# Token softmax on loaded phi, loads in another order, one more chunk by seven products, and weight sums without a wait

## The chip, the cores and the metric

The kernel runs on one NeuronCore of a Trainium2 chip. The time is that of the device for one execution, in microseconds; the median of three runs is given with the lowest and the highest. TensorE (PE) multiplies, ScalarE (ACT), VectorE (DVE) and GpSimd (POOL) do the rest, SyncE (SP) and ScalarE issue the transfers. Each of these queues is worked through in order.

## The reference

Memory attention of 4 batches, 8 heads, 576 tokens and 64 dims with 32 memory slots, then two feed-forward layers over 2304 tokens:

```python
a = exp(phi - max(phi, axis=2)); a = a / (sum(a, axis=2) + 1e-9)      # softmax over the 576 tokens
k_m, v_m = a^T k, a^T v                                               # 32 x 64 a head
attn = softmax(q k_m^T / 8) v_m                                       # softmax over the 32 slots
x = attn with its heads side by side                                  # 2304 x 512
x = ((x w_a) * (x w_b)) w_out                                         # d_ff 1536
h = x w_in; out = (h * sigmoid(1.702 h)) w_out2                       # d_ff 2048
```

All inputs are float32. The kernel gets its precision from pairs: each operand is split into a rounded part and the rest, and a product is three matmuls (`PASSES`).

## The kernel before, in words

An order planner (`Order`, lines 101 to 192) writes the program. Each piece of work is a generator that asks for an engine, with the time at which its inputs are there and an estimated length, or for a buffer slot, or waits for a mark. The planner takes the request that can start first and, among equal ones, the lowest priority number, and so fixes the order of every engine's queue and of the transfers. Estimated lengths are in `Lengths`, `dve`, `act`, `pool`; the estimated landing of a load is in `load` with `RATE0` (bytes per ns, and a delay) and a start value. What the chip then waits for are semaphores between real accesses.

**Units.** There are eight units of attention (batch and half of the heads, four heads each). `memory(n)` (from line 525) takes phi as loaded, tokens on partitions, five columns of tokens (the fifth half full). It brings phi to the layout with (head, slot) on partitions: for units 0 and 1 by 20 small products with the identity (line 552), for the others by a copy into `et` (lines 540, 542) and five transposes (line 549). There it takes the maximum (lines 556 to 560), the exponential with its sum (lines 562 and 566), transposes back (lines 570, 574), copies into `phi`, and multiplies with k and v (line 590). The sum's reciprocal scales the result (lines 597 to 606), line 612 transposes it, and line 629 makes the scores, whose softmax over slots is `softmax`. `queries` (line 509) transposes q.

**First layer.** `fold` (line 792) multiplies the value memories into groups of w_a and w_b, `gated` (line 844) applies that to the attention weights. A fold needs both units of its batch and four weight pieces. The pieces come as `raw` transfers in the order `FIRST`, into six buffers, and are decoded by ScalarE (lines 438, 442) and VectorE (line 444), which frees the buffer. `warm_up` (line 1582) fills TensorE with products of the identity until the first weight group is there. Line 1006 is the product with w_out by Strassen-like sums (seven products instead of eight), line 1281 that with w_in in the same way.

**Last stage.** The 2304 tokens go in nine chunks of 256. Chunks 0 to 3 are plain (`proj2`, line 1482): 2 tiles x 16 weight chunks x 3 passes, 512 columns each. Chunks 4 to 8 go by seven products (`proj2_seven`, line 1513): 7 x 8 x 3 matmuls of 256 columns, in the order P4, P1, P2, P5, P7, P6, P3. For these, `sums_gated` adds blocks of the gated tokens before splitting them, and `load_pair` (line 1445) loads the decoded w_out2 again, makes four differences T1 to T4 for each of eight pairs and splits them. `load_pair` waits for the mark `decoded`, set when all sixteen weight chunks are ready. P4, P5, P7 and P6 use the T blocks, the other products the chunks themselves. The gated tokens of a plain chunk come in quarters (`f_s`), those of a chunk by seven in halves (`fw_s`); the splits go through a ring of six buffers (`sb_s`). Lines 339 and 345 are helpers that record a difference (VectorE or GpSimd) and a rounding copy (ScalarE) for all of these.

## Time and profile before

| | us |
|---|---|
| median of three runs (lowest to highest) | 745.47 (744.72 to 747.44) |
| the profiled execution | 744.51 |
| its span, first to last instruction | 742.7 |
| TensorE busy | 732.1 |
| VectorE, ScalarE, GpSimd busy | 533.2, 430.8, 386.1 |
| granted TensorE clock, mean share of full | 0.999 |

The span is what the trace shows; the execution's time has some 1.8 us around it. Busy TensorE includes the filler products of the first 29 us. The stages end by their lines as follows: folds and gated products at 242 us, line 1006 at 376 us, line 1281 at 551 us, plain chunks at 638 us, chunks by seven at 739 us.

### The profile page before, as it was taken

What the parts mean: (1) busy time and instruction counts of PE and PEld (TensorE: products, weight loads), DVE (VectorE), ACT (ScalarE), POOL (GpSimd) and SP (SyncE); (2) the same over time, 40 slices, a digit from 0 to 9 for tenths busy, and PEclk for the clock granted to TensorE, in tenths of its full rate; (3) what the DMA queues carried; (4) which work ended last, traced back from release to release, by engine and by line L of the source; (5) the groups of instructions that cost most, each with busy time, mean ns of one, the idle gap of its engine ahead of it and who ended that gap; (6) DMA issues with size and microseconds to landing.
All of it is one profiled execution on the core that took longest, in us unless ns stands there. A gap on an engine that the chain in (4) does not pass through costs nothing.

```text
span 742.7 us, 14507 instructions
## 1 busy us (share of the span) xinstructions
PE 732.1 (99%) x5344; PEld 682.7 (92%) x5344; DVE 533.2 (72%) x799; ACT 430.8 (58%) x842; POOL 386.1 (52%) x347
## 2 busy tenths in 40 slices
PE   9899999999999999999999999999999999999997
PEld 8787888888889999999999999999998888999997
DVE  2987777568983447945898666666665697898884
ACT  3678664667863456546866655565656654544441
POOL 0324366447996616914998621333240296776660
PEclk9999999999999999999999999999999999999999
DMA  8998954786778966676525575544699954544411
GB/s 276 343 327 254 322 190 160 224 280 231 256 237 264 313 195 170 171 211 191 186 100 163 180 227 162 163 136 150 210 377 301 328 157 138 189 143 143 143 26 33
DMA packets 110359, 153.53 MB, mean 207 GB/s; under 512 B 8400, under 2 KB 89040, under 8 KB 110288
## 3 DMA queue, kind: packets, MB, share of 16 engines
q1 hardware_dynamic: 104928, 143.13, 60.3%
q10 hardware_dynamic: 5360, 9.47, 3.9%
q8 instruction: 42, 0.69, 0.4%
q14 instruction: 29, 0.24, 0.1%
HBM read 100.01 MB, written 52.56 MB: 205 GB/s over the span
## 4 chain that ended last, share of the span: by engine, by line
PE 92%; DMA 3%; POOL 2%; DVE 2%; SPq 1%; issue 0%; ACT 0%; DVEq 0%; POOLq 0%
PE bank L1281 24%; PE bank L844 21%; PE bank L1006 16%; PE bank L1513 14%; PE bank L1482 12%; PE bank L792 3%; DMA q<-in_q_dram 1%; PE bank L590 1%; DMA raw_p<-in_moe_w_b_dram 1%; DMA kv<-in_k_dram 1%; PE bank L509 1%; POOL w L339 1%; SPq L372 1%; POOL attn L339 1%; DVE attn L339 0%
## 5 line engine op out<-in xcount | busy, mean ns | idle before, releaser
L844 PEld LDWEIGHTS bank<-attn,eff 128*128 128x128 f32 x1152 | 154.3, 188 | 16.2 <-issue 6.1
L844 PE MATMUL bank<-attn,eff 128*128 128x288 f32 x1152 | 163.1, 298 | 0.5 <-DVE eff L812 0.5
L339 POOL TENSOR_TENSOR acc<-acc 128x512 f32<-128x512 f32 (+2 forms) x65 | 95.0, 1481 | 68.2 <-DVE w L339 27.9
L1323 DVE TENSOR_TENSOR acc<-bank,acc 128x384 f32<-128x384 f32 x168 | 89.8, 553 | 46.3 <-PE bank L1281 40.8
L339 DVE TENSOR_TENSOR w<-acc,w 128x512 fp32r<-128x512 f32 (+2 forms) x100 | 105.0, 1076 | 20.5 <-ACT w L345 20.4
L345 ACT ACTIVATE w<-acc 128x512 fp32r<-128x512 f32 (+2 forms) x129 | 74.9, 590 | 65.7 <-PE bank L1513 38.9
L345 ACT ACTIVATE attn<-acc 128x768 fp32r<-128x768 f32 (+2 forms) x80 | 61.0, 769 | 54.5 <-PE bank L1006 38.7
L1006 PE MATMUL bank<-attn,w 128*128 128x384 f32 x504 | 91.8, 335 | 0.8 <-DVE attn L339 0.7
L1006 PEld LDWEIGHTS bank<-attn,w 128*128 128x128 f32 x504 | 87.5, 188 | 2.0 <-DVE attn L339 1.4
L339 DVE TENSOR_TENSOR attn<-acc,attn 128x768 fp32r<-128x768 f32 (+2 forms) x54 | 65.6, 1225 | 31.9 <-ACT attn L345 30.8
L1333 ACT ACTIVATE acc<-acc 128x384 f32<-128x384 f32 x96 | 49.3, 524 | 44.0 <-DVE acc L1323 43.0
L339 POOL TENSOR_TENSOR attn<-acc,attn 128x768 fp32r<-128x768 f32 (+2 forms) x26 | 41.9, 1623 | 35.8 <-ACT attn L345 35.8
L1281 PE MATMUL bank<-attn,w 128*128 128x384 f32 x288 | 55.1, 334 | 0.0
L339 POOL TENSOR_TENSOR w<-dm,w 128x256 fp32r<-128x256 f32 x27 | 24.5, 908 | 57.9 <-ACT w L345 57.9
L888 POOL TENSOR_TENSOR gr<-gr 128x288 f32<-128x288 f32 x48 | 44.6, 931 | 17.0 <-issue 7.0
L339 POOL TENSOR_TENSOR w<-acc,w 128x256 fp32r<-128x256 f32 (+2 forms) x27 | 30.0, 1119 | 44.4 <-ACT w L345 44.3
L1281 PEld LDWEIGHTS bank<-attn,w 128*128 128x128 f32 x288 | 50.4, 188 | 0.0
L1006 PE MATMUL bank<-attn,w1b 128*128 128x384 f32 x252 | 47.6, 336 | 0.2 <-DVE attn L339 0.2
L339 POOL TENSOR_TENSOR sT<-sT,sm 128x576 f32<-128x576 f32 (+1 forms) x12 | 13.5, 1126 | 64.0 <-DVE sm L654 31.7
L1281 PE MATMUL bank<-w1b,w 128*128 128x384 f32 x224 | 46.2, 334 | 0.0
L1006 PEld LDWEIGHTS bank<-attn,w1b 128*128 128x128 f32 x252 | 43.8, 188 | 0.9 <-DVE attn L339 0.5
L1281 PE MATMUL bank<-w 128*128 128x384 f32 x224 | 43.8, 334 | 0.0
(185 smaller groups left out, 1448.9 us busy)
## 6 DMA issues: line engine op xcount, KB each, us to landing
acc<-g1d SPq DMA_DIRECT2D x63, 384.0 KB, 3.8
g2d<-acc SPq DMA_DIRECT2D x96, 192.0 KB, 2.0
raw<-in_moe_w_out_dram SPq DMA_DIRECT2D x24, 512.0 KB, 4.9
acc<-g2d SPq DMA_DIRECT2D x10, 1024.0 KB, 7.6
raw<-in_moe_w_in_dram SPq DMA_DIRECT2D x16, 512.0 KB, 4.3
acc<-g2d SPq DMA_DIRECT2D x16, 512.0 KB, 5.5
g1d<-gr SPq DMA_DIRECT2D x12, 576.0 KB, 4.9
g1d<-acc SPq DMA_DIRECT2D x8, 576.0 KB, 4.8
```

Source lines behind the costliest of these rows:

```text
L339: (nc.gpsimd if e == POOL else nc.vector).tensor_tensor(out=dst, in0=in0, in1=in1, op=op)
L345: nc.scalar.activation(out=hi, in_=src, func=AF.Copy)
L372: nc.sync.dma_start(out=dst.rearrange("p (n f) w -> p n (f w)", n=runs), in_=src)
L792: nc.tensor.matmul(ps[c][0][row(h), :], bdv[b][half, h, :], wt["wab", g, h][0][half, :], start=True, stop=True)
L844: nc.tensor.matmul(dst[:, :U], e[:, c, sw, i * CW + j * P:i * CW + (j + 1) * P], attn(b, mv, c, u * U, U), start=(n == 0), stop=(n == 3 * ...
L888: nc.gpsimd.tensor_tensor(out=dst, in0=in0, in1=in1, op=ALU.subtract)
L1006: nc.tensor.matmul(ps[0][:, :N2], w1_of(a, g, sw)[:, r * P:(r + 1) * P], b[0][:, mv, i], start=(first and q == n == 0), stop=(q == NG1 // ...
L1281: nc.tensor.matmul(ps[0][:, :N2], w[:, sw, r, :], y[mv][r], start=(n == 0), stop=(n == 5))
L1323: nc.vector.tensor_tensor(out=s[0], in0=ps[0][:, :N2], in1=x[0], op=ALU.add)
L1333: nc.scalar.activation(out=c[0], in_=c[0], func=AF.Gelu_apprx_sigmoid)
L1482: nc.tensor.matmul(ps[i, s][0], b[0][:, sw, c - o, :], wo2[c][:, mv], start=(c == n == 0), stop=(c == 4 * K4 - 1 and n == 2),)
L1513: nc.tensor.matmul(ps[name][0][:, :NB], x[0][:, sw, c, :], moving(b, h // 2 + c, mv), start=(h == c == n == 0), stop=(h > 0 and c == K4 - ...
```

## The change

The softmax over tokens stays in the loaded layout: VectorE takes the maximum over the five columns (`mc`, 128 x 128), TensorE transposes it, VectorE reduces it over tokens, makes a diagonal of its negative, and TensorE multiplies a matrix of ones with that diagonal, so that every partition holds the negative maxima. VectorE adds them to phi into `et`, ScalarE takes the exponential in place, VectorE or GpSimd sums over the columns, and TensorE sums over partitions with a product of one column. k and v are multiplied with `et`. The unused half column of `phi` is filled with -3e38 once. `FIRST` and the planner's landing estimate change; chunk 3 goes by seven products; the pairs' sums no longer wait for `decoded`, at a lower priority.

```diff
--- before.py
+++ after.py
@@ -23,7 +23,7 @@
 W1 = 0.0
 HOLD = {}
 PR = 30
-PT = 28
+PT = 31
 MBN = 8
 PA = 10
 HOLDD = {4: ("attn", 1, 0)}
@@ -35,7 +35,7 @@
 PS1 = 14.8
 PT1 = 15
 FRONT = 1.0, 1.0, 1.0
-RATE0 = 300.0, 2500.0
+RATE0 = 335.0, 1700.0
 RATE = 330.0, 3000.0
 PB1 = 4
 PI = 9
@@ -44,11 +44,12 @@
 PW = 5.5
 PY = 5
 RX = 12
+LEAST = -3.0e38
 
 FIRST = (
     ("phi", 0), ("phi", 1), ("kv", 0), ("q", 0), ("kv", 1), ("q", 1), ("raw", 0), ("raw", 1), ("raw", 2), ("raw", 3),
-    ("raw", 4), ("raw", 5), ("phi", 2), ("kv", 2), ("q", 2), ("raw", 6), ("raw", 7), ("phi", 3), ("kv", 3), ("q", 3),
-    ("raw", 8), ("raw", 9), ("raw", 10), ("raw", 11), ("phi", 4), ("kv", 4), ("q", 4), ("phi", 5), ("kv", 5), ("q", 5),
+    ("raw", 4), ("raw", 5), ("phi", 2), ("raw", 6), ("raw", 7), ("kv", 2), ("q", 2), ("raw", 8), ("raw", 9), ("raw", 10),
+    ("raw", 11), ("phi", 3), ("kv", 3), ("q", 3), ("phi", 4), ("kv", 4), ("q", 4), ("phi", 5), ("kv", 5), ("q", 5),
 )
 
 
@@ -114,7 +115,7 @@
 
     def __init__(self):
         self.clock = {PE: 0.0, ACT: 0.0, DVE: 0.0, POOL: 0.0}
-        self.dma, self.marks, self.streams, self.count = 2000.0, {}, [], 0
+        self.dma, self.marks, self.streams, self.count = 2800.0, {}, [], 0
 
         self.handicap = {DVE: W0}
         self.rate, self.land = RATE0
@@ -306,10 +307,12 @@
     zero = pa.tile([P, 1], F32, name="zero")
     bdk = [pa.tile([P, HG * M], F32, name=f"bdk{i}") for i in range(2)]
     phi_s = slots(pa, 2, [P, HG, C0, M], "phi")
-    et_s = slots(pa, 2, [P, C0, SP, 2], "et")
+    et_s = slots(pa, 2, [P, HG, C0, M], "et")
+    mc_s = slots(pa, 2, [P, HG * M], "mc")
+    ones = pa.tile([P, P], F32, name="ones")
     kv_s = slots(pa, 2, [P, 2, HG, C0, D], "kv")
     q_s = slots(pa, 2, [P, QC, D], "q")
-    mx_s = slots(pa, 3, [P, 6], "mx")
+    mx_s = slots(pa, 3, [P, 2], "mx")
     kvn_s = slots(pa, 2, [P, 2, 2, D], "kvn")
     qT_s = slots(pa, 2, [P, HG, U], "qT")
     sT_s = slots(pa, 2, [P, S], "sT")
@@ -528,82 +531,62 @@
         if n in HOLD:
             yield ("mark", *HOLD[n])
         ph = loaded.pop(("phi", n))
...
+        mc = yield "slot", mc_s
+        t, mx = yield DVE, max(t, mc[1]), dve(HG * C0 * M), mx_s
+        m = [mx[0][:, i:i + 1] for i in range(2)]
+        top = mc[0].rearrange("p (h m) -> p h m", h=HG)
+        nc.vector.reduce_max(out=top, in_=ph[0].rearrange("p h c m -> p h m c"), axis=AX.X)
+        t, bb = yield PE, t, 110, bank_a
+        tp, low, kvp, total = (bb[0][:, i * P:(i + 1) * P] for i in range(4))
+        nc.tensor.transpose(tp, mc[0], ident)
+        t, _ = yield DVE, t, dve(P)
+        nc.vector.reduce_max(out=m[0], in_=tp, axis=AX.X)
+        t, _ = yield DVE, t, dve(P)
+        nc.vector.tensor_scalar(out=mc[0], in0=ident, scalar1=m[0], scalar2=-1.0, op0=ALU.mult, op1=ALU.mult)
+        t, _ = yield PE, t, 220
+        nc.tensor.matmul(low, ones, mc[0], start=True, stop=True)
         et = yield "slot", et_s
...
+        t, _ = yield DVE, max(t, et[1]), dve(HG * C0 * M)
+        nc.vector.tensor_tensor(
+            out=et[0], in0=ph[0],
+            in1=low.rearrange("p (h u m) -> p h u m", h=HG, u=1).to_broadcast([P, HG, C0, M]), op=ALU.add,
         )
...
+        phi_s.release(ph, t)
+        t, _ = yield ACT, t, act(HG * C0 * M)
+        nc.scalar.activation(out=et[0], in_=et[0], func=AF.Exp)
+        t2, e = yield {DVE: dve(HG * C0 * M), POOL: pool(4 * P)}, t
+        if e == DVE:
+            nc.vector.reduce_sum(out=top, in_=et[0].rearrange("p h c m -> p h m c"), axis=AX.X)
+        else:
+            for c in range(1, C0):
+                nc.gpsimd.tensor_tensor(
+                    out=top, in0=et[0][:, :, c], in1=et[0][:, :, 0] if c == 1 else top, op=ALU.add
+                )
+        t = max(t, (yield "mark", "kv", n))
         kvs = loaded.pop(("kv", n))
...
         for c in range(C0):
             t, _ = yield PE, t if c == 0 else 0.0, 240
             for h in range(HG):
                 nc.tensor.matmul(
...
+                    kvp[h * M:(h + 1) * M, :], et[0][:, h, c, :], kvs[0][:, :, h, c, :],
                     start=(c == 0), stop=(c == C0 - 1),
                 )
...
+        et_s.release(et, max(t, t2))
         kv_s.release(kvs, t)
+        t2, _ = yield PE, t2, 110
+        nc.tensor.matmul(total[:, :1], mc[0], ones[:, :1], start=True, stop=True)
+        mc_s.release(mc, t2)
         t2, _ = yield DVE, t2, 70
...
+        nc.vector.tensor_scalar_add(m[1], total[:, :1], 1e-9)
         t2, _ = yield DVE, t2, 75
...
+        nc.vector.reciprocal(out=m[1], in_=m[1])
         kvn = yield "slot", kvn_s
         t, e = yield {ACT: act(256, True), DVE: dve(320)}, max(t, t2, kvn[1])
         kv2 = kvp.rearrange("p (i u d) -> p i u d", i=2, u=1).to_broadcast([P, 2, 2, D])
         if e == ACT:
...
+            nc.scalar.activation(out=kvn[0], in_=kv2, func=AF.Copy, scale=m[1])
         else:
...
+            nc.vector.tensor_scalar(out=kvn[0], in0=kv2, scalar1=m[1], scalar2=None, op0=ALU.mult)
         bank_a.release(bb, t)
         mx_s.release(mx, t)
         t, ps = yield PE, t, 220, bank_a
@@ -1194,7 +1177,7 @@
         yield "mark", "front"
         wide = views(acc, 2 * FN, 3, n)
         give(fw_s, wide[:2])
-        yield "mark", "sw", NQ, 0, A22
+        yield "mark", "sw", NF, 0, A22
         give(fw_s, wide[2:])
         for p in range(F2 // P // 2):
             yield "mark", "wt", p
@@ -1338,7 +1321,7 @@
 
 
 
-    NF, NQ, NS, NW = 3, 4, 4, NT // NB
+    NF, NW = 3, NT // NB
 
     def gated_part(s, i, o, e):
         t = 0.0
@@ -1354,13 +1337,12 @@
         loaded["f", i, o] = s, f
 
     QUARTERS = [(i, o) for o in range(0, 4 * K4, K4) for i in range(NF)]
-    QUARTERS += [(i, o) for i in range(NF, NQ) for o in range(0, 4 * K4, K4)]
 
     def load_gated():
         for i, o in QUARTERS:
             s = yield "slot", f_s
             yield from gated_part(s, i, o, o + K4)
-        for i in range(NQ, NW):
+        for i in range(NF, NW):
             for o in (0, 2 * K4):
                 s = yield "slot", fw_s
                 yield from gated_part(s, i, o, o + 2 * K4)
@@ -1384,20 +1366,8 @@
                 t = max(t, (yield "mark", "sb", i, o, s))
             f_s.release(slot, t)
         od.mark(t, "front")
-        for i in range(NQ, NW):
-            yield from (split_whole(i) if i < NS else sums_gated(i))
-
...
     A21 = 7
     MERGE = {
@@ -1447,7 +1417,7 @@
             in_=w2d[2 * p * P:(2 * p + 2) * P, :].rearrange("(k p) f -> p k f", p=P),
         )
         od.load(max(t, m[1]), 2 * P * DM * 4, "pair", p)
-        t = max((yield "mark", "pair", p), (yield "mark", "decoded"))
+        t = yield "mark", "pair", p
         b11, b12, b21, b22 = (x[:, k, j] for k in range(2) for j in range(2))
         n = DM // 2
         for i, (dst, in0, in1) in enumerate(
@@ -1495,7 +1465,7 @@
 
     def proj2_seven(i):
 
-        if i == NS:
+        if i == NF:
             for p in range(2 * K4):
                 yield "mark", "wt", p
         ps, ts = {}, {}
@@ -1606,7 +1576,7 @@
         od.spawn(9, room_last())
         yield from proj2([(i, s) for i in range(NF) for s in range(2)])
         for i in range(NF, NW):
-            yield from (proj2([(i, 0), (i, 1)]) if i < NS else proj2_seven(i))
+            yield from proj2_seven(i)
 
     def quad(g, p):
         for name in ("P1", "P6", "P7", "P5", "P3", "P4", "P2"):
@@ -1615,9 +1585,10 @@
     with tc.manual_schedule():
 
         last = C0 - 1
-        unused = [s[0][:, :, last, :] for s in phi_s.free] + [s[0][:, last] for s in et_s.free]
-        unused += [s[0][:, i, :, last, :] for s in kv_s.free for i in range(2)]
-        for t in [zero, *unused]:
+        for s in phi_s.free:
+            nc.vector.memset(s[0][:, :, last, :], LEAST)
+        nc.vector.memset(ones, 1.0)
+        for t in [zero] + [s[0][:, i, :, last, :] for s in kv_s.free for i in range(2)]:
             nc.vector.memset(t, 0.0)
         make_identity(nc, ident)
         n0 = 2 * NHG
```

## Rows read from the trace of the kernel before

**Rows 1.** The page, part 1: busy us, share of the span, instructions of each engine.
```profile
...
PE 732.1 (99%) x5344; PEld 682.7 (92%) x5344; DVE 533.2 (72%) x799; ACT 430.8 (58%) x842; POOL 386.1 (52%) x347
...
```

**Rows 2.** The page, part 4: the chain that ended last, share by line.
```profile
...
PE bank L1281 24%; PE bank L844 21%; PE bank L1006 16%; PE bank L1513 14%; PE bank L1482 12%; PE bank L792 3%; DMA q<-in_q_dram 1%; PE bank L590 1%; DMA raw_p<-in_moe_w_b_dram 1%; DMA kv<-in_k_dram 1%; PE bank L509 1%; POOL w L339 1%; SPq L372 1%; POOL attn L339 1%; DVE attn L339 0%
...
```

**Rows 3.** TensorE's waits: line, released by which: us in total, times, longest.
```profile
...
PE bank L549 <- POOL et L540: 1.7, 1, 1.7
...
PE bank L509 <- ACT qT L330: 1.2, 1, 1.2
PE bank L1006 <- DVE attn L339: 0.9, 3, 0.5
PE bank L844 <- DVE eff L812: 0.5, 1, 0.5
...
```

**Rows 4.** The chain in order of time: start us, us, what.
```profile
...
64.95 0.55 PE bank L549 x5
65.50 0.44 PE bank L570 x4
...
66.72 0.11 PE bank L574
...
550.67 87.08 PE bank L1482 x384
637.75 100.80 PE bank L1513 x840
...
```

**Rows 5.** TensorE's instructions in order of time: start us, us, instruction, count.
```profile
...
24.55 4.06 PE L1582 MATMUL bank<-ident 128*128 128x128 f32 x34
...
33.33 3.40 PE L844 MATMUL bank<-attn,eff 128*128 128x288 f32 x24
...
39.83 1.30 PE L590 MATMUL bank<-kv,phi 128*32 128x128 f32 x40
...
```

**Rows 6.** Windows: busy us (instructions) of each engine, clock, DMA share, GB/s.
```profile
...
0.00:29.00 29.00, 27.64 (x361) 25.01 (x364) 14.05 (x43) 14.04 (x33) 2.42 (x8) 1.00 0.91 303
29.00:62.00 33.00, 29.11 (x327) 22.38 (x321) 29.77 (x69) 25.21 (x57) 10.90 (x13) 1.00 0.96 316
551.00:573.00 22.00, 22.00 (x99) 18.19 (x98) 10.22 (x16) 10.90 (x20) 0.90 (x1) 1.00 0.97 316
573.00:594.00 21.00, 21.00 (x94) 17.41 (x93) 13.38 (x21) 13.78 (x28) 4.67 (x6) 1.00 0.97 332
594.00:616.00 22.00, 22.00 (x99) 18.22 (x98) 20.83 (x25) 13.02 (x33) 20.90 (x24) 1.00 0.52 149
...
658.00:678.00 20.00, 20.00 (x169) 20.00 (x168) 17.22 (x21) 8.96 (x16) 13.40 (x9) 1.00 0.47 143
...
```

**Rows 7.** VectorE's groups by shape: busy us, mean ns of one, idle before.
```profile
...
L659 DVE TENSOR_REDUCE sm<-sT 128x18 f32<-128x576 f32 x6 | 4.5, 750 | 1.3 <-ACT sT L657 1.1
...
L558 DVE TENSOR_REDUCE mx<-bank 128x1 f32<-128x64 f32 x8 | 1.6, 204 | 0.0
...
```

**Rows 8.** SP's queue in order of time, as in rows 5.
```profile
...
23.00 0.61 SPq L354 DMA_DIRECT2D kv<-in_k_dram  x1
...
```

**Rows 9.** VectorE in order of time, as in rows 5.
```profile
...
24.46 0.69 DVE L444 SCALAR_TENSOR_TENSOR acc<-acc,raw 128x512 uint32<-128x512 uint32 x1
...
38.42 0.69 DVE L444 SCALAR_TENSOR_TENSOR acc<-acc,raw_p 128x512 uint32<-128x512 uint32 x1 [0.40 <-ACT raw_p L442]
...
```

**Rows 10.** GpSimd in order of time, as in rows 5; idle time before it in brackets.
```profile
...
588.12 1.44 POOL L339 TENSOR_TENSOR acc<-acc 128x256 f32<-128x256 f32 x2 [24.91 <-DVE acc L339]
...
620.66 3.82 POOL L339 TENSOR_TENSOR w<-raw,w 128x256 fp32r<-128x256 f32 x4
...
```

**Rows 11.** Line 1445: ns min/median/max, first and last start.
```profile
...
L1445 ACTq EVENT_SEMAPHORE  x9: 17/38/3898, 552.4 to 606.6; - x9
...
```

**Rows 12.** Groups of lines between 573 and 594 us, columns as in rows 7.
```profile
...
L339 DVE TENSOR_TENSOR w<-acc,w 128x512 fp32r<-128x512 f32 x6 | 4.1, 686 | 1.4 <-ACT w L345 1.4
...
```

**Rows 13.** Groups of lines between 594 and 616 us, columns as in rows 7.
```profile
...
L339 DVE TENSOR_TENSOR w<-acc,w 128x512 fp32r<-128x512 f32 x8 | 9.2, 1146 | 1.2 <-ACT w L345 1.2
...
```

More of the change, by code (lines that the diff above doesn't have):

```diff
@@ L543, in memory @@
-        part = 240 if n < NHG else 70
-        t, ba = yield PE, t, part * last, bank_a
-        t1, bb = yield PE, t, part, bank_a
-        for c in range(C0):
-            dst = (ba if c < last else bb)[0][:, c % last * P:(c % last + 1) * P]
-            if n >= NHG:
-                nc.tensor.transpose(dst, et[0][:, c].rearrange("p s x -> p (s x)"), ident)
-                continue
-            for h in range(HG):
-                nc.tensor.matmul(dst[h * M:(h + 1) * M, :], ph[0][:, h, c, :], ident, start=True, stop=True)
@@ L553, in memory @@
-        even = bb[0][:, :P].rearrange("p (s x) -> p s x", x=2)[:, :, 0]
-        t, mx = yield DVE, t, dve(512), mx_s
-        m = [mx[0][:, i:i + 1] for i in range(6)]
-        nc.vector.reduce_max(out=m[0], in_=ba[0], axis=AX.X)
-        t, _ = yield DVE, max(t, t1), dve(64)
-        nc.vector.reduce_max(out=m[1], in_=even, axis=AX.X)
-        t, _ = yield DVE, t, 70
-        nc.vector.tensor_scalar(out=m[2], in0=m[0], scalar1=m[1], scalar2=-1.0, op0=ALU.max, op1=ALU.mult)
-        t, _ = yield ACT, max(t, et[1]), act(512, True) + 190
@@ L562, in memory @@
-        nc.scalar.activation(
-            out=et[0][:, :last].rearrange("p c s x -> p (c s x)"), in_=ba[0], func=AF.Exp, bias=m[2], accum_out=m[3]
-        )
-        t2, _ = yield ACT, t, act(64, True) + 190
-        nc.scalar.activation(out=et[0][:, last, :, 0], in_=even, func=AF.Exp, bias=m[2], accum_out=m[4])
-        t, _ = yield PE, t, 70 * last
-        for c in range(last):
-            nc.tensor.transpose(
-                ba[0][:, c * P:(c + 1) * P], et[0][:, c].rearrange("p s x -> p (s x)"), ident
-            )
@@ L585, in memory @@
+        t = max(t, (yield "mark", "kv", n))
         kvs = loaded.pop(("kv", n))
-        kvp = bb[0][:, 2 * P:3 * P]
         for c in range(C0):
@@ L603, in memory @@
         if e == ACT:
-            nc.scalar.activation(out=kvn[0], in_=kv2, func=AF.Copy, scale=m[5])
+            nc.scalar.activation(out=kvn[0], in_=kv2, func=AF.Copy, scale=m[1])
         else:
-            nc.vector.tensor_scalar(out=kvn[0], in0=kv2, scalar1=m[5], scalar2=None, op0=ALU.mult)
+            nc.vector.tensor_scalar(out=kvn[0], in0=kv2, scalar1=m[1], scalar2=None, op0=ALU.mult)
         bank_a.release(bb, t)
@@ L1386, in split_gated @@
         od.mark(t, "front")
[L1387 to L1400 removed]
+        for i in range(NF, NW):
+            yield from sums_gated(i)
     A21 = 7
```

36 lines of the change are left out of this document (removed).

## The prediction

> **What bounds the kernel now.** I read the page's busy times first, then the chain that ended last, then who waited, and only then the stretches that the change touches. TensorE is busy for 732.1 of 742.7 us [rows 1], and the chain runs over its lines almost alone [rows 2], so what counts is TensorE work taken out and TensorE waits put in. Those waits are small [rows 3]: 1.7 us just before the first gated product at 33.33 us, 1.2 and 0.5 at lines 509 and 844 in the stretch 29 to 62, 0.9 at line 1006 in the middle. The chain in order of time [rows 4] gives the two pieces of the last stage whole: 87.08 us for 384 matmuls of four plain chunks, 100.80 us for 840 of five chunks by seven products, both without a gap. Ahead of 33.33 us TensorE mostly fills time: the 34 rows of line 1582 are products of the identity that nothing reads [rows 5]. That front ends with vector work. Two stretches are crowded beside TensorE [rows 6]: from 29 to 62 us VectorE is busy 29.77 of 33 us with the DMA engines at 0.96, and from 594 to 616 us VectorE 20.83 and GpSimd 20.90 of 22 us. Between 551 and 594 us it is the other way: GpSimd does 5.6 us in 43, VectorE 23.6, and the DMA engines are at 0.97.
>
> **The change, part by part.** The base is the profiled execution's own 744.51 us (span 742.7 and 1.8 around it), 0.96 under the median of 745.47.
>
> *Chunk 3 by seven products.* A plain chunk is 87.08 / 384 = 226.8 ns a matmul, times 96 = 21.77 us. A chunk by seven is 100.80 / 840 = 120.0 ns, times 168 = 20.16 us [rows 4]. Gain 1.61 us, all on the path as long as the chunk's operands are there. The Trainium skill, "TensorE: Matmul & The Clock Gate", section "Back-to-back issue gap", gives an isolated matmul its columns over 2.4 GHz and 2.5 ns. By that the chunk would gain 96 x 215.8 - 168 x 109.2 = 2.4 us; the rows have about 13 ns over the columns in both forms, and decide.
>
> *The token softmax without transposes.* For units 2 to 7 ten transposes each go: 0.55 us at line 549, 0.44 and 0.11 at lines 570 and 574 [rows 4], 6 x 1.10 = 6.60 us. The first five of unit 2 stand in the front's wait and give nothing, which leaves 6.05. Added for each unit: one transpose, 0.11; one full-precision product with the diagonal, two rows of the kind of line 1582 at 4.06 / 34 = 0.119 [rows 5], 0.24; one product of a single column with the same 128 x 128 weights. No row shows that one: between nothing and the 0.24 of the full product; I take 0.20, near the upper end, since the weights are the same size. Sum 0.55 x 6 = 3.3 us. Net gain 6.05 - 3.3 = 2.75 us (2.5 to 3.9). It counts where TensorE has no gaps, from 33 us on. Units 0 and 1 lose 40 matmuls and ten transposes in the front, where fillers take their place: nothing.
>
> *The vector work that comes for it.* A unit now costs VectorE a maximum over 640 values, one over 128, a scalar operation of 128 columns, an addition of 640 and a sum of 640 (or four additions on GpSimd). The nearest rows are 0.75 us for a reduction of 576 and 0.20 for one of 64 [rows 7]. So 0.82, 0.27, 0.25, 0.82, 0.82 = 3.0 us, and if reading every fifth value of a strided line costs twice as much 4.6; at the low end a sum on GpSimd leaves 2.2. What goes is a reduction of 512 and one of 64, a scalar operation and some of the copies, about 1.4. So VectorE gains 0.8 to 3.2 us a unit, while ScalarE loses two accumulator reads, one exponential and copies, about 1 us. The cover is ScalarE, which can take over copies, and GpSimd, busy 10.90 of 33 us [rows 6]. Without it, two units at 1.6 us in a stretch with 3.2 us of free VectorE put some 3 us on TensorE. I take 0, as the row of GpSimd is the larger room.
>
> *The front.* The chain of units 0 and 1 no longer goes through 20 small products, a read of PSUM by ScalarE and two copies back, and VectorE is busy only 14.05 of the first 29 us [rows 6]; the scores of these two units, and with them the softmax that keeps VectorE full up to the first gated product, can come earlier. The reciprocal now stands behind the products with k and v and one more product, some 0.4 us in the chain. The limit is weight piece 3, whose decode decides the first fold. The gated start at 33.33 can move by 3 us at the most (the wait of 1.7 and about as much of filler) and back by 2 (three or four of the new VectorE operations in front of the fold's). I take 1 us earlier.
>
> *The order of loads.* Weight pieces 6 and 7 now stand on SP's queue ahead of unit 2's k, v and q. Piece 6 reuses the buffer of piece 0, whose last read is VectorE at 24.46 to 25.15; the queue issued unit 2's k at 23.00 [rows 8, 9]. So SP waits up to some 2 us with k, v and q of unit 2 queued behind it; TensorE read them at 39.83 [rows 5]. Pieces 10 and 11 need the buffers of pieces 4 and 5, the latter read at 38.42 to 39.11 [rows 9], and hold back phi, k, v and q of unit 3. Against that, the third group of weights arrives sooner, and TensorE has a third block with the tokens at hand. Between a gain of 1.7 us (the waits of lines 509 and 844 gone) and a loss of as much I take 0. No engine but SP is held.
>
> *Sums of the second output weights early.* The eight pairs cost 32 subtractions and 32 splits. Their last lower part ends at 620.66 + 3.82 = 624.5 [rows 10], 13.3 us before TensorE reaches the first chunk by seven at 637.75. Now TensorE gets there after 288 plain matmuls, at 550.67 + 65.3 = 616.0, less the 3.75 us gained ahead: 612.2. So the sums must move by some 12 us relative to the work around them. Room: GpSimd's idle 37 us and VectorE's 19 between 551 and 594 [rows 6] for 64 operations of 0.7 to 1.2 us, some 60; half of them done there bring the end to about 606. The f loads for chunk 3 come when the ring of six split buffers lets the last plain quarter go, as far ahead of use as before. Each pair's load is issued from ScalarE's queue and waits there for its buffer, up to 3.9 us [rows 11]; splits of f and decodes stand behind it. The ring of six splits holds 6 x 12 x 0.227 = 16 us of TensorE work, which covers one such hold-up. Once chunks by seven run, each keeps VectorE 17.22 and GpSimd 13.40 of 20 us [rows 6], so a sixth one holds its pace. I take 0, with a loss of up to 10 us at the other end.
>
> Sum: 1.61 + 2.75 + 1.0 = 5.4 us. 744.5 - 5.4 = **739.1 us**.
>
> **The rivals.** *The sums come too late.* Place: the start of chunk 3 at 612 us. For: before, GpSimd stood idle for 25 us up to 588 with pairs loaded, since its next sum waited for one on VectorE [rows 10]; both engines were full until the end; and the subtractions of the splits took 686 ns beside an idle GpSimd, 1146 ns beside a busy one [rows 12, 13]. Waking GpSimd up early would stretch the 37 VectorE operations between 551 and 594 us [rows 6] by about 0.46 each, 17 us, and leave VectorE no room: all 64 then take GpSimd's time, about 1 us each from 562, to 626 us, less 3.75 gained ahead: 622. TensorE would stand 10 us and more: 739.1 + 10 to 12 = 749 to 751. The Trainium skill states the mechanism in "SBUF — State Buffer", section "Who interferes with whom": a VectorE instruction with two inputs in SBUF and a GpSimd instruction that reads SBUF exclude each other. By that rule this rival is the likelier; the trace agrees on the stretching, but GpSimd's and VectorE's work did overlap in time at the longer durations. Against: only products P4, P5, P7, P6 need these sums, and P1 and P2, which don't, stand between. It decides from a stall of 5.4 us, an end at about 618.
>
> *VectorE becomes the bound in the front.* For: 29.77 of 33 us busy. The added work costs 3 us between 29 and 62, or the order of loads costs 2, and the front gains nothing: 744.5 - 4.4 + 3 = 743 us. Within 0.5%.
>
> *The front gives all it has.* First gated product at 30.3, waits of 1.7 us gone: 744.5 - 4.4 - 3 - 1.7 = 735 us.
>
> *The change does not reach the path.* The queues' order is written anew from changed costs, and other waits of the middle (0.9 us before line 1006) grow by the 4.4 us that the parts bring: 744.5, within 0.5%.
>
> **How the numbers follow.** Forecast 0.51 (range of its own 736.5 to 742.5), VectorE in the front 0.16, gains lost in the middle 0.10, sums late 0.12, the front gives all 0.11. A run of this kernel can tell about 0.5% from no change, 3.7 us about 745.47: faster is below 741.7, slower above 749.2. Faster: 0.9 of the forecast and the last, and some of the front's case, 0.60. Slower: most of the late sums and a bad front, 0.12. The rest, 0.28, is the same. Range 735 to 747: below it a twelfth, above it an eighth.
>
> **What would show it.** Right: the chain has three plain chunks of 21.8 us and six of 20.2 with nothing between; lines 549, 570 and 574 gone and 0.55 us of new matmuls a unit; the first gated product between 31 and 33 us; TensorE's busy time down by about 4 us from there on; the last lower part of the pairs before 612 us. Wrong: a TensorE wait at the first product by seven on a split of the pairs or of chunk 3; waits of TensorE between 33 and 75 us above 4 us; a first gated product after 34.5 us.

## The result, and the profile after

The changed kernel takes 755.73 us (median of four runs, 752.27 to 757.73) against 746.46 of the kernel before beside it: a ratio of 1.0127, 95% interval 1.0104 to 1.0151. It is slower by some 9 us. 739.1 was forecast, with a range of 735 to 747.

The profiled execution took 754.17 us, its span is 752.4, against 744.51 and 742.7. First the page's busy times, which answer to [rows 1].

```profile
PE 734.2 (98%) x5314; PEld 684.1 (91%) x5314; DVE 554.1 (74%) x820; ACT 428.4 (57%) x814; POOL 397.4 (53%) x362
```

TensorE is busy 2.1 us longer with 30 fewer matmuls. Its waits (line, released by: us in total, times, longest) answer to [rows 3].

```profile
PE bank L1483 <- ACT w L348: 4.3, 2, 2.3
PE bank L547 <- DVE mc L545: 1.5, 1, 1.5
...
PE bank L541 <- DVE mc L538: 1.2, 2, 0.7
...
PE bank L1452 <- DVE w L342: 1.0, 2, 0.5
...
PE bank L577 <- POOL mc L562: 0.5, 2, 0.3
```

Lines 1452 and 1483 are the plain chunks and the chunks by seven; 538 to 577 belong to the new softmax. The chain in order of time (start, us, what), as [rows 4]:

```profile
552.79 32.70 PE bank L1452 x144
585.52 0.68 DVE w L342
...
612.73 2.38 DVE w L342 x2
615.13 0.36 SPq L1333
615.55 0.33 issue
615.89 8.44 DMA acc<-g2d
624.34 1.61 DMA out_dram<-dm
625.98 0.57 ACT w L348
626.59 121.76 PE bank L1483 x996
```

The chain leaves TensorE at 585 us and comes back to it at 626.59. Stage by stage: the folds and gated products end at 244.39 us (242.25 before), line 1264 starts at 378.07 where its predecessor 1281 started at 375.95, so the middle keeps its length, and the last stage runs from 552.79 to 748.35, 195.6 us against 187.9. So in these two profiles the front is 2.1 us longer and the last stage 7.7. The forecast had the front 3.75 shorter and the last stage 1.6. The 7.7 is clear. The 2.1 is not: the profiles below whose front is that of the kernel before end it anywhere from 242.16 (e7) to 245.48 (e8), so what the front costs has to come from medians.

What happens at the start of chunk 3 stands in three queues. TensorE, start, us, instruction, idle time before it:

```profile
616.70 3.33 PE L1452 MATMUL bank<-w1b,w 128*128 128x512 f32 x14
621.99 0.50 PE L1483 MATMUL bank<-w1b,w 128*128 128x256 f32 x2 [1.96 <-ACT w L348]
...
626.59 3.23 PE L1483 MATMUL bank<-w 128*128 128x256 f32 x12 [2.29 <-ACT w L348]
```

ScalarE beside it (line 348 splits, line 333 copies results out of PSUM):

```profile
621.31 1.15 ACT L348 ACTIVATE w<-acc 128x512 fp32r<-128x512 f32 x2 [6.07 <-DMA acc<-g2d]
622.37 0.58 ACT L333 ACTIVATE acc<-bank 128x512 f32<-128x512 f32 x1
625.43 0.60 ACT L333 ACTIVATE dm<-bank 128x512 f32<-128x512 f32 x1 [2.48 <-DMA out_dram<-dm]
625.92 1.66 ACT L348 ACTIVATE w<-acc 128x512 fp32r<-128x512 f32 x3
```

SP's queue, of the changed kernel and, behind it, of the kernel before (lines 1333 and 1350 load the gated tokens):

```profile
615.13 1.65 SPq L1333 DMA_DIRECT2D acc<-g2d  x2
616.88 9.96 SPq L1538 DMA_DIRECT2D out_dram<-dm  x12
```
```profile
590.13 5.76 SPq L1350 DMA_DIRECT2D acc<-g2d  x2
...
626.26 5.25 SPq L1350 DMA_DIRECT2D acc<-g2d  x4
```

The halves of chunk 3 lie in the memory of the last plain quarters, so their load can go out only when VectorE has finished the splits of those, at 615.10. TensorE's plain work is over at 620.03. That leaves 4.9 us for a load that takes 6 to 8 and a split. Before, the first load for a chunk by seven went out at 626.26 for a use at 637.75, 11.5 us ahead. The first split waits for the load until 621.31; then a result copy that waits for an output store holds ScalarE, with the next split behind it, until 625.43. In the chain above that store stands behind the same load: 8.44 us of the second half's transfer, then 1.61 of the store. The wait also costs clock. Windows (busy us of PE, PEld, DVE, ACT, POOL with instructions, then granted clock, DMA share, GB/s):

```profile
622.00:626.00 4.00, 2.08 (x12) 1.57 (x12) 2.34 (x2) 1.52 (x4) 1.29 (x1) 0.74 0.68 227
626.00:630.00 4.00, 3.41 (x14) 3.18 (x15) 3.43 (x4) 3.40 (x8) 2.65 (x2) 0.50 0.65 175
630.00:634.00 4.00, 4.00 (x33) 4.00 (x32) 4.00 (x3) 1.79 (x4) 4.00 (x3) 0.91 1.09 360
```

0.50 is the lower of the clock's two levels, 1.2 GHz of 2.4. Of the last stage's 9.3 us over 186.3 (65.3 for three plain chunks and 121.0 for six by seven) the plain part has 1.9, TensorE's idle time at 620 to 627 us 4.5, and 2.9 are left. Most of that goes with the lower clock: busy time times the missing share of the clock comes to some 2.6 us over the three windows.

The front, as [rows 6] and [rows 7] (the groups: busy us, mean ns of one, idle before):

```profile
0.00:29.00 29.00, 27.34 (x292) 24.58 (x292) 18.20 (x42) 12.32 (x25) 3.92 (x10) 1.00 0.86 279
29.00:62.00 33.00, 27.82 (x285) 21.60 (x289) 31.38 (x62) 23.20 (x48) 13.88 (x17) 0.95 0.96 309
```
```profile
L447 DVE SCALAR_TENSOR_TENSOR acc<-acc,raw_p 128x512 uint32<-128x512 uint32 x8 | 9.1, 1146 | 0.1
...
L538 DVE TENSOR_REDUCE mc<-phi 128x128 f32<-128x640 f32 x6 | 7.8, 1303 | 0.5 <-DMA phi<-in_phi_dram 0.5
...
L550 DVE TENSOR_TENSOR et<-phi,bank 128x640 f32<-128x640 f32 x6 | 4.8, 802 | 0.0
```

VectorE is at 31.38 of 33 us, TensorE's busy time there has fallen from 29.11 to 27.82, and of the gated products one stands at 32.29, where 32.3 was forecast, and the others behind a wait for VectorE from 33.50 on.

### The profile page after: what moved, and what is told of

Read it like the earlier page. It is cut to its first block, busy times and chain, and to the rows that moved or that the text cites. A ratio compares the mean times of both kernels' runs of the same rounds, so it can differ in the third digit from the quotient of the medians.

```text
span 752.4 us, 14465 instructions
## 1 busy us (share of the span) xinstructions
PE 734.2 (98%) x5314; PEld 684.1 (91%) x5314; DVE 554.1 (74%) x820; ACT 428.4 (57%) x814; POOL 397.4 (53%) x362
## 4 chain that ended last, share of the span: by engine, by line
PE 84%; DVE 6%; DMA 4%; issue 2%; POOL 2%; ACT 1%; SPq 1%; ACTq 0%; DVEq 0%; POOLq 0%
PE bank L1264 23%; PE bank L827 19%; PE bank L1483 16%; PE bank L989 16%; PE bank L1452 4%; PE bank L775 2%; DMA phi<-in_phi_dram 1%; DMA acc<-g2d 1%; DVE w L342 1%; DVE attn L342 1%; PE bank L1548 1%; DMA raw_p<-in_moe_w_a_dram 1%; DVE acc L447 1%; DMA kv<-in_v_dram 1%; POOL mc L562 1%
## 5 line engine op out<-in xcount | busy, mean ns | idle before, releaser
L827 PE MATMUL bank<-attn,eff 128*128 128x288 f32 x1152 | 166.6, 300 | 1.2 <-DVE eff L795 1.0
L342 POOL TENSOR_TENSOR acc<-acc 128x512 f32<-128x512 f32 (+2 forms) x73 | 110.0, 1530 | 63.3 <-DVE w L342 35.2
L342 DVE TENSOR_TENSOR w<-acc,w 128x512 fp32r<-128x512 f32 (+2 forms) x109 | 113.9, 1072 | 22.7 <-ACT w L348 22.6
L348 ACT ACTIVATE w<-acc 128x512 fp32r<-128x512 f32 (+2 forms) x139 | 80.0, 587 | 66.9 <-PE bank L1483 46.1
L348 ACT ACTIVATE attn<-acc 128x768 fp32r<-128x768 f32 (+2 forms) x85 | 62.9, 748 | 54.8 <-PE bank L989 38.2
L342 DVE TENSOR_TENSOR attn<-acc,attn 128x768 fp32r<-128x768 f32 (+3 forms) x60 | 69.6, 1168 | 33.2 <-ACT attn L348 31.8
L1483 PE MATMUL bank<-attn,w 128*128 128x256 f32 x288 | 42.4, 283 | 0.0
```

Of the source, the lines that this page charges most:

```text
L342: (nc.gpsimd if e == POOL else nc.vector).tensor_tensor(out=dst, in0=in0, in1=in1, op=op)
L348: nc.scalar.activation(out=hi, in_=src, func=AF.Copy)
L827: nc.tensor.matmul(dst[:, :U], e[:, c, sw, i * CW + j * P:i * CW + (j + 1) * P], attn(b, mv, c, u * U, U), start=(n == 0), stop=(n == 3 * ...
L1483: nc.tensor.matmul(ps[name][0][:, :NB], x[0][:, sw, c, :], moving(b, h // 2 + c, mv), start=(h == c == n == 0), stop=(h > 0 and c == K4 - ...
```

## The experiments

All are compared with the kernel before on the same chip, whose medians were 746.4 to 746.8 us. Two leave something out that the result needs, and give another result: e5 (the differences of the weights) and e9 (the right groups of five).

| run | median us | ratio (95%) |
|---|---|---|
| e1_front_only | 747.64 | 1.0019 (1.0006 to 1.0032) |
| e2_last_only | 753.14 | 1.0091 (1.0056 to 1.0125) |
| e3_softmax_only | 751.93 | 1.0082 (1.0057 to 1.0106) |
| e4_order_only | 749.55 | 1.0042 (1.0028 to 1.0057) |
| e5_no_sums | 749.50 | 1.0047 (1.0028 to 1.0066) |
| e6_own_buffer | 749.88 | 1.0047 (1.0027 to 1.0067) |
| e7_plain3_wait | 754.62 | 1.0115 (1.0091 to 1.0139) |
| e8_early_only | 748.58 | 1.0032 (1.0018 to 1.0047) |
| e9_contig | 746.28 | 1.0000 (0.9988 to 1.0012) |
| e10_pairwise | 750.30 | 1.0060 (1.0043 to 1.0077) |
| e11_own_timed | 744.86 | 0.9978 (0.9963 to 0.9993) |
| e12_full_mend | 749.53 | 1.0046 (1.0028 to 1.0065) |
| e13_timed_only | 749.07 | 1.0046 (1.0027 to 1.0064) |
| e14_full_own_timed | 746.81 | 1.0010 (0.9999 to 1.0021) |
| e15_own_pool_queue | 753.37 | 1.0102 (1.0081 to 1.0122) |
| e16_own_sp_queue | 746.52 | 0.9999 (0.9984 to 1.0015) |
| e17_timed_pool_queue | 749.77 | 1.0050 (1.0033 to 1.0068) |
| e18_timed_sp_queue | 743.22 | 0.9974 (0.9960 to 0.9987) |

**The two halves.** e1 is the changed kernel with the old last stage:

```diff
-    NF, NW = 3, NT // NB
+    NF, NQ, NS, NW = 3, 4, 4, NT // NB
...
-        t = yield "mark", "pair", p
+        t = max((yield "mark", "pair", p), (yield "mark", "decoded"))
```

> The changed front (token softmax, order of loads, landing estimate) with the last stage as it was: four plain chunks, sums after all sixteen weight chunks. Theory of two separate losses: the first layer ends 2.1 us later in the changed kernel (244.4 against 242.25 us), the rest is lost between 594 and 628 us, so this one is 1 to 3 us slower than before, 747 to 749 us. Rival, that the front is innocent and only moves the last stage's plan: within 1 us of before or faster by up to 2.5.

e2 is the kernel before with the new last stage, the same edit the other way round.

> The changed last stage (three plain chunks, six by seven products, sums of the weights without the wait, at priority 31) with the front as it was. Theory of two separate losses: 6 to 9 us slower than before, 752 to 755 us, with TensorE waiting 4 to 6 us at the first products by seven. Rival, that the shifted front spoils the plan of the last stage: not slower, 743 to 746 us.

The last stage alone loses 6.8 us, the front alone 1.4: most of the loss is in the last stage, and the sum falls 1 us short of the whole. Against the forecast's 3.75 and 1.6 us of gain, the front misses by some 5 us and the last stage by some 8.

**Parts of the last stage.** e7 is e2 with the sums still waiting, e8 is the kernel before with early sums and nothing else. The line below is taken out in e8 and put back in e7, with the priority that belongs to it:

```diff
-        t = yield "mark", "pair", p
+        t = max((yield "mark", "pair", p), (yield "mark", "decoded"))
```

> Three plain chunks and six by seven products on the front of before, but the pairs' sums wait for the last weight chunk as before. If early sums help at all, the sums end near 622 us, 6 us after TensorE is ready for chunk 3, and it is slower than with them: 755 to 760 us. Rival, that early sums do the harm by holding ScalarE's queue: faster than with them, 747 to 751 us.

> Only the sums without the wait (priority 31), four plain chunks as before. Theory that a plain chunk more hides the late splits: within 1 us of before. Rival, that the early sums hold ScalarE's queue and starve the plain chunks: 1 to 3 us slower with waits at line 1482.

e7's time lies between the two expectations, and its 1.5 us over e2 are within the noise. It has 7.0 us of waits at the first products of chunk 3, but not the same ones as the change. SP's queue and TensorE:

```profile
608.38 0.99 SPq L1350 DMA_DIRECT2D acc<-g2d  x2
```
```profile
616.31 0.51 PE L1500 MATMUL bank<-w1b,w 128*128 128x256 f32 x2 [0.41 <-ACT w L345]
...
625.94 0.58 PE L1500 MATMUL bank<-w 128*128 128x256 f32 x1 [3.27 <-ACT w L345]
627.18 0.80 PE L1500 MATMUL bank<-w 128*128 128x256 f32 x2 [0.66 <-DVE w L339]
```

The load for chunk 3 goes out 7.5 us ahead of TensorE's use, and the first product waits 0.4 us. In e2 the load goes out at 614.56, 4.9 us ahead. So early sums hold back the plain splits that free the memory by some 6 us. The last two waits of e7, 3.9 us together, end with a split of a pair on ScalarE (625.47 to 625.89) and the pair's lower part on VectorE (625.92 to 627.13): there the sums themselves are late. Both orders lose, each by its own mechanism. Early sums alone, with four plain chunks, cost 2.4 us (e8).

e5 leaves out the pairs' work and keeps their loads:

```diff
-            t = yield from combine(t, dst, in0, in1, ALU.subtract, n)
-            od.spawn(PT, split_t(t, wo2_t[p][i], dst, p, i))
...
-            return wo2_t[p][{T1: 0, T3: 1, T2: 2, T4: 3}[b]][:, mv]
+            b = {T1: B11, T3: B21, T2: B22, T4: B22}[b]
```

> The changed last stage on the front of before, with the subtractions and splits of the eight weight pairs left out (64 VectorE or GpSimd operations and 32 of ScalarE); the pairs are still loaded, and P4, P5, P7, P6 multiply with blocks of the weights in their place. Theory that the pairs' work holds back the last splits of the plain chunks, and with them the load of chunk 3 that goes into the same buffers: no wait at the start of chunk 3, 743 to 746 us. Rival, that the load is too late in any case, since it waits for the ring of six splits: a wait of 3 to 5 us stays, 748 to 751.

With VectorE and GpSimd relieved of all of it, the load for chunk 3 goes out at 606.87, 17 us ahead of use (TensorE is itself some 6 us late there), and the chunk starts without a wait, though it lies in the same memory. So it takes both, the shared memory and the pairs' work, to make the load late. But the kernel is still 3.5 us slower, and the wait now stands in the plain chunks: 3.1 us for a split on ScalarE at 578 us. ScalarE's rows there (the last column is idle time before) show why. The loads of the pairs are issued from its queue and wait for their buffer, with everything behind them:

```profile
560.01 7.09 ACTq L1432 DMA_DIRECT2D acc<-w2d  x4
567.15 0.66 ACT L438 ACTIVATE dm<-raw 128x512 f32<-128x512 f32 x1 [13.09 <-DMA acc<-w2d]
577.05 0.38 ACTq L1432 DMA_DIRECT2D acc<-w2d  x1
577.48 1.67 ACT L345 ACTIVATE w<-acc 128x512 fp32r<-128x512 f32 x3 [5.50 <-DMA w2d<-dm]
```

e6 is e2 with chunk 3's halves in buffers that no plain quarter uses (the plain quarters keep two):

```diff
-        give(f_s, views(acc, FN, 3, 2 * AN))
+        give(f_s, views(acc, FN, 2, 2 * AN + FN))
...
-        for c, x in enumerate(views(acc, FN, 2, n), len(pieces) - 3):
+        wide = views(acc, 2 * FN, 3, n)
+        for c, x in enumerate(wide[:2], len(pieces) - 3):
             yield "mark", "raw", c
-            give(f_s, [x])
+            give(fw_s, [x])
```

> The changed last stage on the front of before; both halves of chunk 3 get buffers that no plain quarter uses (4 of the 6 quarter buffers go for it, 2 stay), so that their load does not wait for the last plain splits. Theory of the shared buffers: the load lands before 612 us and the wait at the start of chunk 3 goes; 6 us less than without it, 745 to 748 us, if two quarter buffers feed the plain chunks. Rival, that the work on the pairs itself is late: the wait stays at 3 to 4 us, on splits of chunk 3 or of the pairs, 751 to 754.

The wait at chunk 3 is gone: the stretch by seven is one piece of 120.96 us. Half of the loss is left, 2 us more than was expected, in the plain part: 1.8 us of wait at 593, and behind it the lower clock.

```profile
592.97 2.25 PE L1467 MATMUL bank<-attn,w 128*128 128x512 f32 x6 [1.77 <-ACT w L345]
```
```profile
590.00:594.00 4.00, 2.13 (x9) 1.15 (x8) 3.46 (x7) 3.25 (x7) 1.23 (x2) 1.00 0.94 318
594.00:598.00 4.00, 4.00 (x11) 3.08 (x11) 1.27 (x3) 0.88 (x2) 0.49 (x1) 0.58 0.94 314
```

**Parts of the front.** e3 is the softmax without the order of loads, e4 the order (`FIRST`, `RATE0`, the start value) without the softmax.

```diff
-RATE0 = 300.0, 2500.0
+RATE0 = 335.0, 1700.0
...
-    ("raw", 4), ("raw", 5), ("phi", 2), ("kv", 2), ("q", 2), ("raw", 6), ("raw", 7), ("phi", 3), ("kv", 3), ("q", 3),
+    ("raw", 4), ("raw", 5), ("phi", 2), ("raw", 6), ("raw", 7), ("kv", 2), ("q", 2), ("raw", 8), ("raw", 9), ("raw", 10),
```

> Only the token softmax without transposes; loads, landing estimate and last stage as before. Theory that vector work eats the front's gain (reductions of 640 values took 1.29 us, VectorE busy 79.9 instead of 70.9 of 86 us from 26 to 112): 0 to 3 us slower. Rival, that the order of loads does the harm: 1 to 2.5 us faster than before, since about 0.5 us of TensorE goes for each of units 2 to 7.

> Only the order of loads and the planner's landing estimate, softmax and last stage as before. Theory that vector work eats the gain: within 1.5 us of before. Rival, that the order of loads does the harm (SP waits for buffers of undecoded weight pieces with k, v, q behind): 2 to 4 us slower, with phi, k, v, q of unit 3 issued 8 us later than before.

Each alone costs more (about 6 and 3 us) than both together (1.4); for e3 neither theory had that. Part of it, about 2.7 us in each profile, is not in the front at all but at the w_out stage (line 989 or 1007), whose order is written anew and then waits for GpSimd. The parts of the front don't add.

e9 lets both reductions read their 640 values in the order in which they lie:

```diff
-        nc.vector.reduce_max(out=top, in_=ph[0].rearrange("p h c m -> p h m c"), axis=AX.X)
+        nc.vector.reduce_max(out=mc[0], in_=ph[0].rearrange("p h c m -> p (h c m)").rearrange("p (x c) -> p x c", c=C0), axis=AX.X)
```

> The changed front with the old last stage, as in e1_front_only, but the maximum and the sum over the five columns read the same 640 values in the order in which they lie, five neighbours a result (the results are those of other groups, so the softmax is another; instructions and sizes are the same). Theory: it is the stride of 32 values between the five that makes the reduction 1.29 us; in order it takes 0.75 to 0.85 as the reduction of 576 does, VectorE is relieved by some 5 us between 26 and 112 us, and since VectorE bounds that stretch the time goes from 747.6 to 745 to 746.5, that is to or below the kernel before. Rival 1: the duration comes from the 128 results with five values each, not from the stride: it stays at 1.2 to 1.3 and nothing moves. Rival 2: the duration falls but VectorE is not what holds TensorE there: the time stays at 747.3 to 748.

```profile
L538 DVE TENSOR_REDUCE mc<-phi 128x128 f32<-128x640 f32 x6 | 4.8, 796 | 0.5 <-DMA phi<-in_phi_dram 0.5
```

796 ns in place of 1303, and the time goes from 1.0019 of before to 1.0000. So the stride cost some 1.4 us in all, though the two intervals just touch, and the front still gives nothing back.

e10 takes four operations with two inputs for one reduction:

```diff
-        nc.vector.reduce_max(out=top, in_=ph[0].rearrange("p h c m -> p h m c"), axis=AX.X)
+        for c in range(1, C0):
+            nc.vector.tensor_tensor(
+                out=top, in0=ph[0][:, :, c], in1=ph[0][:, :, 0] if c == 1 else top, op=ALU.max
+            )
```

> The changed front with the old last stage, but the maximum over the five columns, and the sum where VectorE makes it, by four operations of 128 columns with two inputs instead of one strided reduction. Theory: about 0.2 us each, 0.8 in place of 1.29, so half of the relief of e9_contig at the least and a time of 746 to 747; the result is the reference's. Rival: four instructions with two inputs cost 0.3 each and more beside GpSimd, 1.2 in all, and the time stays at 747.6.

The four took 384 + 3 x 489 ns = 1.85 us, not 0.8, and the time rose to 750.3. That is the rival, and more than it: one strided reduction took 1.30. The 0.2 us for each were an estimate; no row had shown a chain of such operations.

**Mends of the last stage.** e11 is e6 with the request for a pair's load made at the planned time at which its buffer is free:

```diff
         m = yield "slot", tb_s
+        t, _ = yield ACT, max(t, m[1]), 40.0
```

> The changed last stage with the old front and with chunk 3 in buffers that no plain quarter uses (as in e6_own_buffer, 749.9), and each load of a pair put on ScalarE's queue only at the planned time at which its buffer is free. Theory: what is left of the loss in e6_own_buffer comes from ScalarE's queue standing at those loads, with the splits of the plain chunks behind it (a wait of 1.8 us at 593 and a granted clock of 0.97 from 551 to 600). With that gone the last stage has no wait, takes 187 to 188.5 us, and the time is 746 to 747, no better than the kernel before by more than the 1.6 us of the seventh chunk form: 745 at the best. Rival: the splits are late because VectorE and GpSimd are crowded by the pairs' sums, wherever the loads stand: the wait moves but stays, 749 to 750.

e13 has this without the buffers of its own (an edit of e2), e14 is the whole change with both mends, e12 adds e10's operations to e14. They cost 2.7 us there, as in e10 against e1.

> The changed last stage with the old front, with the pair loads put on ScalarE's queue at the planned time, but chunk 3 again in the buffers of the last plain quarters (e2_last_only, 753.1, with the one mend of the queue). Theory A, both causes are needed: the splits of the last plain quarters still end by the pace of VectorE and GpSimd, the load of chunk 3 is issued behind them and a wait of 3 to 5 us stays at the first product by seven: 748 to 751. Theory B, the queue alone: with the splits no longer behind waiting loads the last quarter is split some 5 us earlier, the f load goes out earlier by as much, and the time is that of e11_own_timed, 744.9 to 746. Theory C, the buffers alone: nothing is gained over e2_last_only, 752 to 754, and the gain from e6_own_buffer to e11_own_timed came from the order written anew.

> The whole change, strided reductions and all, with the two mends of the last stage (buffers of its own for chunk 3, pair loads at the planned time). Theory: front and last stage add; e11_own_timed has 744.9, the changed front alone was 747.6 against 746.8, so 745.5 to 746.5, against 755.7 of the change as it was. Rival: the order of the middle is written anew and gives up more, as in e3_softmax_only and e4_order_only: 748 to 750.

> The whole change with three mends: chunk 3 in buffers of its own, pair loads at the planned time, column maxima and sums by operations of two inputs. Theory: the losses are separate and add: the front at +0 to +0.8, the last stage as e11_own_timed, so within 0.8 us of that run, 745.5 to 747.5, against 755.7 of the change. Rival: the parts disturb one another through the order that is written anew (as the softmax alone and the order of loads alone did in the middle): 748 or more.

Neither mend alone does half: 1.0091 without them, 1.0047 and 1.0046 with one, 0.9978 with both. With both, the whole change comes to 746.81 where it was 755.73, so 8.9 us of the result are these two. What is left between e11 and e14, 0.9978 and 1.0010, came with the front; their last stages have no wait.

But ScalarE still stood idle for 6.0 us before the first pair load in e11, as in e6 (6.6), and the planner had written another order behind the moved request. To part the two, e15 and e16 keep e6's order of computation on every engine and issue the pair loads from another queue:

```diff
-        nc.scalar.dma_start(
+        nc.gpsimd.dma_start(
```

> As e6_own_buffer (749.9), every engine's order of computation unchanged, but the eight pair loads are issued from GpSimd's queue, so that nothing of ScalarE stands behind a load that waits for its buffer. GpSimd has little to do up to 594 us. Theory A, the hold of ScalarE's queue: its 6.6 us of idle time at 555 to 562 us goes, the split that TensorE waits 1.8 us for at 593 us comes in time, and the run ends at 745 to 746.5, as e11_own_timed. Theory B, the order: what counted in e11_own_timed was the order written anew behind the moved request, not the hold; then the wait at 593 stays and the time with it, 749 to 750.

> The same with the pair loads on SP's queue. ScalarE is free of them, but SP has the loads of the weight pieces and of the gated tokens behind a load that waits. Theory A of e15_own_pool_queue: ScalarE's hold goes, but the gated tokens' loads are held by as much, so between 745 and 749, above e15_own_pool_queue. Theory B: the wait at 593 stays, 749 to 750, or grows.

e16, the same edit with `nc.sync`, brings e6's 1.0047 to 0.9999, with the order of computation untouched. ScalarE in e6 and, behind it, the same split in e16:

```profile
560.33 1.44 ACTq L1430 DMA_DIRECT2D acc<-w2d  x2
561.81 0.67 ACT L442 ACTIVATE raw<-raw 128x512 uint32<-128x512 uint8 x1 [6.60 <-DMA g2d<-acc]
562.38 0.62 ACT L345 ACTIVATE w<-acc 128x512 fp32r<-128x512 f32 x1
```
```profile
555.62 0.63 ACT L345 ACTIVATE w<-acc 128x512 fp32r<-128x512 f32 x1
```

The 6.6 us of idle time are gone, the wait of TensorE near 593 us falls from 1.8 to 1.3, and the clock behind it, 0.58 in e6, is 1.00. So ScalarE's hold is the cause of most of what was left in e6. On GpSimd's queue the hold hits worse, though that engine had the time: an issue counts 0.72 us there, its queue stood 8.7 us for the first buffer, and the sums behind the loads came late (4.4 us of TensorE's wait on ScalarE, 1.8 on VectorE, in the plain part).

e17 and e18 put e11's loads on GpSimd's and on SP's queue. e17 loses again, with a wait of 3.0 us for VectorE in the plain part.

> e11_own_timed (744.9) with the pair loads on GpSimd's queue. There ScalarE still stood idle for 6.0 us at 556 to 562 us before the first pair load, without a wait of TensorE behind it. Theory A: nothing left to gain, 744.5 to 745.2. Theory B: the loads wait behind GpSimd's sums later on and come late, 746 or more.

> e11_own_timed (744.9) with the pair loads on SP's queue, where they cost little in e16_own_sp_queue. Theory A: the plain part has no wait left in e11_own_timed, so nothing is to be gained, 744.5 to 745.3. Theory B: freeing ScalarE of its 6.0 us of idle time before the first pair load brings the splits forward and the granted clock stays full: 744 or less. Rival: the loads of the gated tokens behind the pair loads come late, 746 to 747.

e18 has the lowest median, 743.22 us, 0.9974 of the kernel before. That it is faster than e11 (0.9978) is not shown: their intervals lie almost on each other, and ScalarE's 6.0 us of idle time in e11 had no wait of TensorE behind it. Its chain through the last stage:

```profile
550.62 65.32 PE bank L1468 x288
615.95 120.96 PE bank L1499 x1008
```

SP issues the two loads for chunk 3 there 14.0 us ahead of use, instead of 4.9:

```profile
601.97 1.12 SPq L1348 DMA_DIRECT2D acc<-g2d  x2
```

## Why the prediction was wrong

*Chunk 3 by seven, 1.61 us: right as a term.* 65.32 + 120.96 = 186.28 us in e18 against 187.88 before, 1.60 less. In the change as made it was overrun.

*Sums early, at 0: this step failed, in two sentences.* "The f loads for chunk 3 come when the ring of six split buffers lets the last plain quarter go, as far ahead of use as before": the lead went from 11.5 to 4.9 us. TensorE now reaches the chunk 17.7 us sooner (620.03 for 637.75), but the splits that free the memory end only 11.1 us sooner (615.10 for 626.24). With the sums waiting (e7) they end at 608.3, without sums (e5) at 606.8: it is the early sums that hold them. All runs that give chunk 3 other memory (e6, e11, e12, e14 to e18) have no such wait. e2, e13 and the change have it, e7 in part; e5, without the sums, has not. "The ring of six splits ... covers one such hold-up": it did for the 3.9 us of [rows 11], with the order that ScalarE had then. The longest wait of a pair's load was 4.4 us in the change and 6.0 in e5, and e16 shows what the holds cost behind the new order. I had named the load and the hold, and put each at nothing.

*The rival of late sums had the place (the start of chunk 3), by the wrong mechanism.* It had a stall of 10 to 12 us; 4.5 were measured. GpSimd ends the pairs' last lower part at 614.56, ahead of TensorE's 620:

```profile
611.35 3.21 POOL L342 TENSOR_TENSOR w<-raw,w 128x256 fp32r<-128x256 f32 x3
```

TensorE waited for the splits of chunk 3. The rival's point of decision was about 618, and the sums met it. Its mechanism is to be seen in e7, where the sums still wait: 3.9 us.

*Vector work, at 0: failed as a cover.* The size was right: between 26 and 112 us the new lines of six units take 18.7 us of VectorE and those that went took 8.1, so 1.8 a unit, within my 0.8 to 3.2. (The "some 3 us" without a cover do not follow: two units at 1.6 just fill the 3.2 us that were free.) "I take 0, as the row of GpSimd is the larger room" was wrong: GpSimd took the sums of five of these units and ScalarE the copies of q, and VectorE rose from 70.88 to 79.87 us all the same. About 4.5 of these 9 us are its decodes with two inputs, half of which took 1146 ns instead of 740 [rows 9 show one at 0.69]. Why they do so is not settled: with the softmax or the order of loads alone they took 757 to 830. The strided maximum was put at 0.82, with twice that as the upper bound; it took 1.30. (It reads every 32nd value, not every fifth.) A rule that I did not weigh bears on it. The Trainium skill, "Vector Engine (DVE) Microarchitecture Reference", section "Measured stream behaviour on trn2 (trn3 not measured)", has the full rate only for runs of two or more adjacent words and, for a bitwise program with two sources, 1.73 ns a column instead of 1.05 where one source hops at every element. The trace agrees roughly: 1303 - 796 = 507 ns for 640 values is 0.79 ns a value more, where the page has 0.68.

*Softmax without transposes, 2.75: the instructions were about right.* At the full clock the chain has 0.22 us for line 547, 0.17 for line 541 and 0.13 to 0.38 for line 577, so 0.5 to 0.8 a unit (0.55 forecast). The gain is not to be seen in the time. In the change's profile the waits on VectorE and GpSimd at lines 541, 547 and 577 come to 3.2 us. Its clock of 0.65 at 34 to 38 us is no sign of the change, as e11 has 0.62 there with the old front. What stands in the way in e9, where the stride is gone, stays open: its rows have smaller waits at the same lines, and 1.5 us for the load of q.

*The front, 1 us earlier: wrong in effect.* One gated product came at 32.29, 1.0 us earlier; the stream of them begins at 33.50, 0.2 later than before, since VectorE was not ready. *The order of loads, 0:* 3.1 us lost by itself, 4.7 gained with the softmax (1.0082 in e3 to 1.0019 in e1); 2.7 us of each lie at the w_out stage.

*By "What would show it"*: the wait at the first product by seven on a split of chunk 3 was named as the sign against, and it came. The pairs' last lower part, wanted before 612, came at 614.56. The other signs against stayed away: the waits between 33 and 75 us come to 3.3 us, under the 4, and the first gated product came before 34.5.

## What to carry to other kernels

Where a consumer is moved forward, ask of each of its loads which buffer it takes, who frees that, and by whose pace; the lead of the load before use is one subtraction in the trace, and it is the number to forecast. A load issued from a computing engine's queue stops that engine when its buffer is late (ScalarE for 6.6 us in e6); give it to a queue that has nothing urgent behind it. When an engine is nearly full, do not count on room on a neighbour to cover work added to it: here it did not. And a short wait of TensorE can cost more than itself, since the clock may fall behind it (2.9 us beside 4.5 of waits here).

## What the runs showed of the hardware

- Behind waits of TensorE of 1.8 us (e6) and 2.3 us (the change) the granted clock was 0.58 and 0.50 in the next window of 4 us.
- The same wait does not always bring it. The old front waits 1.7 us ahead of the first gated product in each of its profiles; between 34 and 38 us the profile of the kernel before then has a clock of 1.00 and that of e11 0.62, and their fronts end at 242.25 and 244.69 us:

```profile
34.00:38.00 4.00, 4.00 (x35) 3.94 (x33) 3.80 (x10) 3.52 (x11) 2.39 (x3) 1.00 1.04 333
```
```profile
34.00:38.00 4.00, 4.00 (x22) 4.00 (x21) 3.18 (x10) 2.86 (x7) 2.34 (x3) 0.62 1.02 331
```

- A chain of four VectorE operations of 128 columns, each reading the result of the one before, took 291 ns apiece at the least and up to 1131 (e10).
- An issue of a pair's load counts 0.72 us on GpSimd's queue (e15), about 0.37 on ScalarE's or SP's (e6, e16).
